# A list scheduler with due times gives way to a written order, in a kernel of memory attention and an erf-softplus FFN

## The chip, the cores and the metric

The kernel runs on 1 core of a Trainium2 chip. The metric is device time in microseconds (us) of one execution; 704.22 us is the median of three runs before the change.

## The reference, cut to what matters

```python
# q, k, v: (8 batches, 8 heads, 576, 64); phi: (8, 8, 576, 32); w_in: (512, 2048); w_out: (2048, 512)
a = exp(phi - max(phi, axis=2)); a = a / (sum(a, axis=2) + 1e-9)
k_m = einsum('bhsm,bhsd->bhmd', a, k)
v_m = einsum('bhsm,bhsd->bhmd', a, v)
scores = matmul(q, k_m.T) / sqrt(64)
attn = exp(scores - max(scores)); attn = attn / (sum(attn) + 1e-9)
x = matmul(attn, v_m)              # as (4608 tokens, 512)
h = x @ w_in
g = h * erf(softplus(h))
out = g @ w_out
```

The result is wanted in float32, so nearly every large product is made of three products of high and low parts.

## The kernel before

The kernel never forms `x`. For each batch `b` it multiplies `v_m` into `w_in` (`vw`, `vw_sums`, through `heads`, line 652: small tiles of 64 x 32) and then the attention weights with that (line 850 for batches 0 and 1, in halves of 288 tokens: `ffn1`; line 756 from batch 2 on: `quad`, seven products for two steps). A step `i` is one of 16 blocks of 128 hidden columns of one of 8 batches, 128 in all. Step by step follow `softplus`, `erf`, `g_split` (product with h, then a high and a low part) and `ffn2` (line 935: four token blocks `d` of 128 rows, accumulated in `pso` over 16 steps); the 64 tokens left over of two batches go together (`ffn2_rest`, `psr`). `memories` makes `k_m` and `v_m` (`sums`, line 598), `attention` the weights. The first four steps of `ffn1` and the first eight of `ffn2` are exact products of float32 rather than three.

The weights come from the host as 64-bit numbers of the same values. `decode` turns one block of w_in or w_out back: a "top" cast bf16 to f16 (line 485), a "low" multiply (lines 486 on ScalarE, 488 on VectorE) and a merge on VectorE (line 480). w_in is stored again in DRAM for the later batches. The pool `wo` has nine buffers for raw and split weights, and both halves of the first q.

The program is written as operations with a cost, a rank (100 x the step at which they are due, some shifted), what they read and write, and one or two "ways", engines that can do them. `Plan.order` then builds the order: a list scheduler that keeps a model of time per engine, of free buffers (`room`, `MOST`, `LEAST`) and of TensorE's clock; at each turn it takes the operation that can begin first, by rank among those that are near. On TensorE it goes on with "small" products as long as there are some. `SHIFT` moves the rank of single operations. The order of the list is the order on each engine. `fill` puts products of zeros (line 414) on TensorE where the model sees it idle in the start.

Of the kernel before, what the change touches and what calls it, by code (L numbers as in the profile page):

```python
# [41 lines left out]
SHIFT = {  # L42
    "at_sums": {
        ("s", 2): 2, ("s", 3): 2,
    },
    "attention": {
        (0,): 12, (2,): 4.5, (3,): 1,
    },
    "decode": {
        ("in", 0): -9, ("in", 1): -10.5, ("in", 2): -12, ("in", 5): -11, ("in", 7): -11, ("out", 2): 11.5,  # L50
        ("out", 3): -14, ("out", 7): -0.5,
    },
    "ffn2_rest": {
        ("s", 0, 2): 5.5, ("s", 10, 2): -5.5, ("s", 12, 2): 3.5, ("s", 6, 2): 2, (7, 0, 2): -14,
    },
    "g_split": {
# [4 lines left out]
    },  # L61
    "memories": {
        (1,): 1.5, (2,): 4,
    },
    "split_wo": {
        (0,): 13, (4,): 4.5, (6,): 6,
    },
    "vw": {
        (0, 4, False): 1.5, (0, 6, False): -9.5, (1, 1, False): 0.5, (1, 5, False): 5, (1, 6, False): -5.5,
    },  # L70
    "vw_sums": {
        ("s", 3): -6.5, (2, 0): 8, (2, 1): 2.5, (2, 3): -1,
    },
}


class Op:
    def __init__(self, ways, rank, kind, nbytes, edge):
        self.ways, self.rank, self.kind, self.nbytes, self.edge = ways, rank, kind, nbytes, edge
        self.engine = next(iter(ways))  # L80
        self.before, self.after, self.tiles, self.placed = set(), [], set(), []
        self.ready = self.start = self.end = 0.0
        self.fill = 0
# [19 lines left out]

class Plan:
# [3 lines left out]
    SIGNAL = 60.0  # L108
    TABLE = 1283.0
    SWITCH = 98.0  # L110
    RELOAD = 170.0
    NEAR = 100.0

    def __init__(self, room, any_order, least, shared):
        self.ops, self.seen = [], {}
        self.room, self.any_order, self.least, self.shared = room, any_order, least, shared
        self.pool_of, self.users, self.turn = {}, {}, {}

    def tile(self, pool, *key):
        self.pool_of[key] = pool  # L120
        self.users[key] = []
        self.turn.setdefault(pool, []).append(key)
        return key

    shift = 0

    def op(self, engine, cost, rank, reads, writes, emit, kind=None, nbytes=0, edge=None, after=(),
           holds=(), other=()):
        x = Op({engine: (cost, emit), **dict(other)}, rank, kind, nbytes, edge)
        x.shift = self.shift  # L130
        x.before.update(after)
        for w, keys in ((False, reads), (True, writes)):
            for k in keys:
                k, part = (k[0], k[1]) if isinstance(k[0], tuple) else (k, None)
                x.tiles.add(k)
# [18 lines left out]
        for k in x.tiles:  # L154
            if k in self.users:
                self.users[k].append(x)
                x.placed.append(k)
        x.placed += [k for k in holds if k not in x.tiles]
        self.ops.append(x)
        return x  # L160

    def order(self):
        n_wait = {}
        for x in self.ops:
            x.rank += 100 * x.shift
            n_wait[x] = len(x.before)
            for y in x.before:
                y.after.append(x)
        room, turn = dict(self.room), dict.fromkeys(self.turn, 0)
        left = {k: len(u) for k, u in self.users.items()}  # L170
        waiting = {e: [x for x in self.ops if e in x.ways and not n_wait[x]] for e in ENGINES}
        free = dict.fromkeys(ENGINES, 0.0)
        table, at_edge, small = None, True, False
        landed, clock, filling = 2200.0, Clock(), True
        releases, out, now, held = [], [], 0.0, set()

        def fits(x):
            need = {}
            for k in x.placed:
                if k in held:  # L180
                    continue
                p = self.pool_of[k]
                if p not in self.any_order and self.turn[p][turn[p] + need.get(p, 0)] != k:
                    return False
                need[p] = need.get(p, 0) + 1
            if any(room[p] < n for p, n in need.items()):
                return False
            return not any(p in self.least for p in need) or self.shared >= sum(
                max(n, self.room[p] - room[p] + need.get(p, 0)) for p, n in self.least.items())

        def best_way(x):
            return min(x.ways, key=lambda e: max(free[e], x.ready, now) + x.ways[e][0])

        while len(out) < len(self.ops):
            best = None
            for e, xs in waiting.items():
                can = [x for x in xs if fits(x)]
                if e == ACT and not at_edge:
                    can = [x for x in can if x.kind != "exp"]
                can = [x for x in can if len(x.ways) == 1 or best_way(x) == e]  # L200
                if not can:
                    continue
                t0 = max(free[e], now, min(x.ready for x in can))
                near = [x for x in can if x.ready <= t0 + self.NEAR]
                if e == PE and small and any(x.kind == "small" and x.ready <= t0 for x in near):
                    near = [x for x in near if x.kind == "small" and x.ready <= t0]
                x = min(near, key=lambda x: x.rank)
                t = max(free[e], x.ready, now)
                if best is None or t < best[0]:
                    best = (t, x, e)  # L210
            if releases and (best is None or releases[0][0] <= best[0]):
                now, _, p = heapq.heappop(releases)
                room[p] += 1
                continue
            if best is None:
                raise RuntimeError(f"nothing fits after {len(out)} of {len(self.ops)}")
            now, x, e = best
            x.engine, (cost, x.emit) = e, x.ways[e]
            for w in x.ways:
                waiting[w].remove(x)  # L220
            for k in x.placed:
                if k not in held:
                    held.add(k)
                    room[self.pool_of[k]] -= 1
                    turn[self.pool_of[k]] += 1
# [16 lines left out]
            elif e == ACT:  # L242
                if x.kind is not None and x.kind != table:
                    cost += self.TABLE
                    table = x.kind
                if x.edge is not None:
                    at_edge = x.edge
                late = 75.0
            elif e == DVE:
                late = 60.0  # L250
            x.cost = cost
            free[e] = now + cost
            x.start, x.end = now, now + cost + late
            if e == SP:
                begin = max(now + 900, landed)
                landed = begin + x.nbytes / (250 if x.nbytes < 1.2e5 else 340 if begin < 13000 else 385)
                x.end = landed + 900
            out.append(x)
            for y in x.after:
                n_wait[y] -= 1  # L260
                y.ready = max(y.ready, x.end + self.SIGNAL)
                if not n_wait[y]:
                    for w in y.ways:
                        waiting[w].append(y)
            for k in x.tiles:
                if k in left:
                    left[k] -= 1
                    if not left[k]:
                        end = max(u.end for u in self.users[k]) + self.SIGNAL
                        heapq.heappush(releases, (end, len(out) * 16 + len(releases), self.pool_of[k]))  # L270
# [4 lines left out]
def tile_memory_attention_then_erf_softplus_ffn(  # L275
# [11 lines left out]
    nc = tc.nc  # L287
# [20 lines left out]
    GB, WB, IB, VB = 3, NPR + 1, 3, 3  # L308
    SLOTS = 31
    MOST = {"h": 14, "e": 12, "at": 14, "sc": 4, "phiT": 3, "uv": 3, "dk": 2, "rr": 3}  # L310
# [858 lines left out]
```

## Time and profile before

| | |
|---|---|
| runs before | 704.22 us median (703.86 to 704.79) |
| the profiled execution | 704.14 us, of which 702.3 us are its span |
| TensorE, VectorE, ScalarE busy | 691.8, 581.8, 541.9 us of the span |
| granted TensorE clock, mean | 0.998 |

The span is the time from the first to the last instruction. PE is TensorE's products, PEld its weight loads, DVE VectorE, ACT ScalarE, POOL GpSimd, SP the engine whose queue issues the DMAs. In rows on instructions the columns are the start and the time in us, the engine, the line of the program, the operation, what is written from what, its shape and how many there are; in brackets the idle time of the engine ahead of it, and who ended it.

### The profile page before, as it was taken

Reading aid. Unit: us, or ns where it says so; the run is one execution under the profiler, and the core shown is the slowest. Engines: PE = TensorE matmul, PEld = TensorE weight load, DVE = VectorE, ACT = ScalarE, POOL = GpSimd, SP = SyncE. Lnnn points to the kernel's source line nnn. Section 1 sums busy time; section 2 is a strip of 40 time slices with the busy share of each in tenths; the row PEclk is TensorE's granted clock in tenths of the full one; section 3 lists DMA queues with packets and bytes.
Section 4 is the critical chain, followed back from the end, with each engine's and each line's share of the span. In section 5 each row is a group of like instructions: output and inputs, shape, how many; then the busy total and the mean of one; then the engine's idle time right before and its main releaser. Section 6 shows DMA issues by size and latency. Waiting matters only on the chain.

```text
span 702.3 us, 13828 instructions
## 1 busy us (share of the span) xinstructions
PE 691.8 (99%) x5204; PEld 549.8 (78%) x5204; DVE 581.8 (83%) x1202; ACT 541.9 (77%) x978; POOL 30.6 (4%) x70
## 2 busy tenths in 40 slices
PE   8999999999999999999999999999999999999997
PEld 3566678778878888888878888788888888888885
DVE  3999999988878889998987997789998898767750
ACT  4689987977777887888878996589987895686831
POOL 0111210000000000000000000000000000011220
PEclk9999999999999999999999999999999999999999
DMA  8999953861736336273634346445321434330002
GB/s 324 415 393 421 378 186 105 289 238 34 256 106 214 102 123 227 76 236 91 250 119 139 99 147 229 128 133 191 117 76 66 122 100 139 98 110 1 1 1 75
DMA packets 71283, 115.07 MB, mean 164 GB/s; under 512 B 38064, under 2 KB 46256, under 8 KB 71216
## 3 DMA queue, kind: packets, MB, share of 16 engines
q1 hardware_dynamic: 71216, 114.18, 47.3%
q8 instruction: 41, 0.67, 0.4%
q14 instruction: 26, 0.21, 0.1%
HBM read 93.19 MB, written 20.97 MB: 163 GB/s over the span
## 4 chain that ended last, share of the span: by engine, by line
PE 90%; DMA 3%; DVE 3%; ACT 2%; SPq 1%; issue 1%; ACTq 0%; DVEq 0%
PE pso L935 48%; PE psh L756 19%; PE psh L850 7%; PE psr L935 6%; PE psa L652 6%; PE psa L598 2%; DMA q<-qT 2%; DMA phiT<-phiT 2%; PE idle L414 1%; DVE sv L677 1%; PE psa L620 0%; ACT wv L403 0%; SPq L442 0%; DVE wv L405 0%; DVE e L887 0%
## 5 line engine op out<-in xcount | busy, mean ns | idle before, releaser
L935 PE MATMUL pso<-wo,g 128*128 128x512 f32 x1440 | 392.6, 395 | 0.0
L935 PEld LDWEIGHTS pso<-wo,g 128*128 128x128 f32 x1440 | 250.4, 188 | 41.7 <-issue 7.3
L756 PEld LDWEIGHTS psh<-at,wv 128*128 128x128 f32 x1008 | 168.6, 188 | 36.5 <-DVE h L677 1.8
L756 PE MATMUL psh<-at,wv 128*128 128x288 f32 x1008 | 190.9, 298 | 1.2 <-ACT g L904 0.4
L872 ACT ACTIVATE e<-h 128x576 f32<-128x576 f32 x128 | 87.0, 685 | 38.8 <-DVE h L677 31.0
L887 DVE TENSOR_TENSOR e<-e,h 128x576 f32<-128x576 f32 x120 | 88.9, 749 | 19.7 <-ACT e L877 19.4
L905 DVE TENSOR_TENSOR g<-e,g 128x576 fp32r<-128x576 f32 x120 | 89.7, 750 | 0.6
L877 ACT ACTIVATE e<-e 128x576 f32<-128x576 f32 x128 | 84.1, 676 | 0.4
L677 DVE TENSOR_TENSOR uv<-uv,psh 128x288 f32<-128x288 f32 x96 | 43.1, 449 | 19.0 <-PE psh L756 15.8
L677 DVE TENSOR_TENSOR h<-uv,psh 128x288 f32<-128x288 f32 x96 | 43.1, 449 | 13.6 <-PE psh L756 13.0
L904 ACT ACTIVATE g<-e 128x576 fp32r<-128x576 f32 x68 | 46.5, 684 | 8.6 <-PE pso L935 4.1
L935 PE MATMUL psr<-wo,rr 128*128 128x512 f32 x192 | 49.5, 393 | 0.0
L850 PE MATMUL psh<-at_hi,vw 128*128 128x288 f32 x224 | 45.1, 306 | 0.8 <-DVE sc L798 0.8
L771 ACT ACTIVATE uv<-psh 128x288 f32<-128x288 f32 x96 | 38.9, 405 | 8.8 <-PE psh L756 8.0
L872 ACT ACT_TABLE_LOAD x33 | 42.3, 1283 | 3.9 <-DVE h L677 3.4
L877 ACT ACT_TABLE_LOAD x33 | 42.3, 1283 | 0.6
L935 PEld LDWEIGHTS psr<-wo,rr 128*128 128x128 f32 x192 | 34.8, 188 | 6.8 <-issue 0.4
L850 PEld LDWEIGHTS psh<-at_hi,vw 128*128 128x128 f32 x224 | 35.0, 188 | 5.9 <-issue 2.1
L914 POOL CAST rr<-g 128x64 fp32r<-128x64 f32 x32 | 14.0, 447 | 579.9 <-DVE g L903 550.6
L652 PE MATMUL psa<-wi,vm 64*32 64x256 f32 x1024 | 37.1, 383 | 0.0
L984 ACT ACTIVATE ot<-pso 128x512 f32<-128x512 f32 x32 | 18.5, 604 | 20.0 <-PE pso L935 19.7
L403 ACT ACTIVATE wv<-sv 128x512 fp32r<-128x512 f32 x48 | 27.8, 624 | 5.6 <-DVE sv L677 5.3
(88 smaller groups left out, 809.8 us busy)
## 6 DMA issues: line engine op xcount, KB each, us to landing
wi<-w_in_d SPq DMA_DIRECT2D x56, 512.0 KB, 4.6
kv<-kv SPq DMA_DIRECT2D x32, 640.0 KB, 9.1
q<-qT SPq DMA_DIRECT2D x16, 576.0 KB, 6.9
out<-ot SPq DMA_DIRECT2D x32, 256.0 KB, 3.5
w<-w_in SPq DMA_DIRECT2D x8, 1023.8 KB, 14.4
w<-w_out SPq DMA_DIRECT2D x8, 1023.8 KB, 13.6
rr<-rest_d SPq DMA_DIRECT2D x28, 256.0 KB, 3.4
rest_d<-g SPq DMA_DIRECT2D x104, 64.0 KB, 1.7
```

What stands on the lines that cost most here:

```text
L403: lambda: nc.scalar.activation(get_hi(), get_src(), AF.Identity))
L652: nc.tensor.matmul(out=get(ps[par])[p * M : (p + 1) * M, m * n : (m + 1) * n], lhsT=w[rows, p, :], rhs=get(x)[rows, p, :], start=True, sto ...
L677: op(DVE, on_dve(n) + extra, rank, reads, [o], lambda: nc.vector.tensor_tensor(out=get_o(), in0=get_x(), in1=get_y(), op=kind))
L756: nc.tensor.matmul(out=get(ps[o]), lhsT=lhsT, rhs=rhs, start=(n < 4 and m == 0), stop=(m == 2), skip_group_check=n >= 4)
L771: lambda x=x: nc.scalar.activation(get(uv)[:, x], get(ps[x]), AF.Identity))
L850: nc.tensor.matmul(out=get(ps), lhsT=x[:, g, k % 2 * P : (k % 2 + 1) * P], rhs=y[:, g, :], start=(n + g == 0), stop=(n == len(parts) - 1 a ...
L872: last[:] = [op(ACT, on_act(S), rank, [("h", i)], [e], lambda: nc.scalar.activation(get(e), get(("h", i)), AF.Softplus), kind="softplus", ...
L877: last[:] = [op(ACT, on_act(S), rank, [e], [e], lambda: nc.scalar.activation(get(e), get(e), AF.Erf), kind="erf", edge=edge, after=last)]
L887: op(DVE, on_dve(S), rank, [e, h], [to if i >= FR2 else (t, 0)], lambda: nc.vector.tensor_tensor(out=get(t)[:, 0].bitcast(F32) if i < FR2 ...
L904: other={ACT: (on_act(S), lambda: nc.scalar.activation(get(t)[:, 0], get(e), AF.Identity))})
L905: op(DVE, on_dve(S), rank, [e, (t, 0)], [(t, 1)], lambda: nc.vector.tensor_tensor(out=get(t)[:, 1], in0=get(e), in1=get(t)[:, 0].bitcast(F ...
L935: nc.tensor.matmul(out=o, lhsT=y, rhs=z, start=(start and n == 0), stop=(stop and n == len(parts) - 1))
```

## The change

`Plan.order` builds no order any more. `WRITTEN` is a text of 3500 numbers in base 32. All operations are sorted by rank (no `SHIFT`); each number takes the operation at position n >> 1 of those that are left, and n & 1 says which of its ways. Models of room and of readiness go; the model of time stays, for the fillers.

Besides: the top cast of `decode` may go to ScalarE; `JOIN` ties the `sums` of batch b + 1 and the first `heads` of `vw_sums` of batch b (2 to 6) into one operation; the last store is cut in two halves of 256 columns, one evicted on ScalarE and stored by SP, one on VectorE and stored from ScalarE's queue; two planning costs are other numbers.

```diff
-SHIFT = {
...
+DIGITS = "ABCDEFGHIJKLMNOPQRSTUVWXYZabcdefghijklmnopqrstuvwxyz0123456789+-"
+WRITTEN = (
+    "lejcCAiUAACAkOGEEClEACAAheieGGCKCCOGGMNLKGJGCECECCECOSOOOUOhEhECQhAhACOcCaMChHWKhDKKEChHaMMWAjAQUZKKUhXhUESCe"
...
+def numbers(text):
+    n = 0
+    for c in text:
+        d = DIGITS.index(c)
+        n = 32 * n + d % 32
+        if d < 32:
+            yield n
+            n = 0
...
+        if join:
+            (was, first), x.rank = x.ways[engine], max(x.rank, rank)
+            x.ways[engine] = (was + cost, lambda: (first(), emit()))
...
+        left, out = sorted(self.ops, key=lambda x: x.rank), []
+        free, landed = dict.fromkeys(ENGINES, 0.0), 2200.0
+        clock, filling, small, table = Clock(), True, False, None
+        for n in numbers(WRITTEN):
+            x = left.pop(n >> 1)
+            e = list(x.ways)[n & 1]
+            cost, x.emit = x.ways[e]
+            now = max([free[e]] + [y.end for y in x.before])
...
-    MOST = {"h": 14, "e": 12, "at": 14, "sc": 4, "phiT": 3, "uv": 3, "dk": 2, "rr": 3}
-    LEAST = {"h": 4, "e": 4, "at": 7, "sc": 3, "phiT": 2, "uv": 1, "dk": 1, "rr": 2}
+    SHARED = ("h", "e", "at", "sc", "phiT", "uv", "dk", "rr")
...
         op(DVE, 1330, rank, [(key, "top")], [(key, "top")],
-           top(lambda y, x: nc.vector.tensor_copy(out=y, in_=x)))
+           top(lambda y, x: nc.vector.tensor_copy(out=y, in_=x)),
+           other={ACT: (2250, top(lambda y, x: nc.scalar.activation(y, x, AF.Identity)))})
...
+    def partner(what, b, c=0):
+        if what == "vw" and c == 0 and JOIN <= b < B - 1:
+            return small["sums", b + 1]
+        
+        return None
...
+        if o == ("psr", B - 1):
+            n = DM // 2
+            half = [slice(0, n), slice(n, DM)]
+            op(ACT, on_act(n, True), rank - 30, [o], [(t, 0)],
+               lambda: nc.scalar.activation(get(t)[:, half[0]], get(o)[:, half[0]], AF.Identity))
+            op(DVE, on_dve(n), rank - 30, [o], [(t, 1)],
+               lambda: nc.vector.tensor_copy(out=get(t)[:, half[1]], in_=get(o)[:, half[1]]))
+            to = out.rearrange("(b s) d -> b s d", b=B)[B - 2 :, S - REST :]
+            op(SP, 60, rank, [(t, 0)], [], lambda: nc.sync.dma_start(
+                out=to[:, :, half[0]], in_=get(t)[:, half[0]]), nbytes=P * n * 4)
+            op(ACT, 600, rank, [(t, 1)], [], lambda: nc.scalar.dma_start(
+                out=to[:, :, half[1]], in_=get(t)[:, half[1]]))
+            return
```

How the text is read: its first number is 190, so position 95, first way. In the sorted list the loads stand first (ranks from -2000), then `memories` (-1000), the scores (-800) and so on, and position 95 is the `zeros` memset of rank 0. The second number, 124, is position 62 of the rest, a one-column memset of a weight tile; the third and fourth, 2 and 0, are the loads of the second and the first `phiT`. So the opening reads, engine by engine (half 1 of q is u = 1):

- SP: phiT 1, phiT 0, k 0, k 1, q 0, q 1, v 1, v 0, w_in 0, 1, 2, 3, store of w_in 0, w_out 0, phiT, w_in 4, w_in 5, store of w_in 1, w_out 1, store of w_in 2, phiT, w_out 2. Before: phiT 0, 1, k 0, 1, q 0, w_in 0, v 0, 1, q 1, w_in 1, w_out 0, w_in 2, w_out 1, w_in 3, w_out 2.
- VectorE from the scores on: two transposes of half 0, one of half 1, maximum 0, transpose 1, maximum 1, subtractions 1 and 0, sum 1, small ones, sum 0, product 1, low multiply of w_in 0, product 0, merge of w_in 0, last transpose 1, low and merge of w_in 1, last transpose 0, low of w_in 2 and w_in 3, merge of w_in 2, merge of w_in 3, top cast of w_out 0.
- ScalarE: top casts of w_in 0, 1, 2 and 3, with the evictions of `heads` 0 behind the second and those of `heads` 1 behind the third.
- TensorE: both scores and the sums of v in one, `heads` of w_in 0, one `ffn1` half, `heads` of w_in 1, six halves, `heads` 3, one half, `heads` 2, eight halves of steps 4 to 7, then `ffn2` of step 0: sixteen halves ahead of the first `ffn2`, where before there were twelve.

In the whole text the second way is taken 118 times: 62 casts of g on ScalarE (before 68), 14 h of `quad` on VectorE (16), 13 h of `ffn1` on ScalarE (17), 15 low multiplies on VectorE (3), 11 top casts on ScalarE (none), 3 copies of the first `phi` on ScalarE (2). Products of small tiles stand in 45 groups, three of them ahead of the first `ffn1`. ScalarE's functions change table 90 times.

## Rows read from the trace of the kernel before

**Rows 1.** The page: the span, part 1 (busy us, share, instructions) and of part 2 what the DMA engines moved in each of 40 equal slices.

```profile
span 702.3 us, 13828 instructions
PE 691.8 (99%) x5204; PEld 549.8 (78%) x5204; DVE 581.8 (83%) x1202; ACT 541.9 (77%) x978; POOL 30.6 (4%) x70
...
GB/s 324 415 393 421 378 186 105 289 238 34 256 106 214 102 123 227 76 236 91 250 119 139 99 147 229 128 133 191 117 76 66 122 100 139 98 110 1 1 1 75
```

**Rows 2.** Busy time of each engine by stretch: the stretch, its length, busy us and instructions of each, granted clock, share of the DMA engines, GB/s.

```profile
31.15:43.20 12.05, 11.12 (x57) 9.20 (x55) 11.69 (x20) 11.16 (x19) 1.36 (x8) 1.00 1.02 375
43.20:100.00 56.80, 56.77 (x417) 35.55 (x418) 54.48 (x80) 50.33 (x81) 12.48 (x20) 1.00 0.97 365
100.00:176.00 76.00, 75.16 (x646) 62.46 (x648) 69.50 (x141) 62.70 (x103) 0.00 (x0) 1.00 0.48 160
```

**Rows 3.** TensorE's products by line over the whole span: busy us and mean ns of one, then the idle time ahead of them and who ended it.

```profile
L756 PE MATMUL psh<-at,wv 128*128 128x288 f32 x1008 | 190.9, 298 | 1.2 <-ACT g L904 0.4 <-ACT bias L521 0.3 <-DVE wv L405 0.3
L850 PE MATMUL psh<-at_hi,vw 128*128 128x288 f32 x224 | 45.1, 306 | 0.8 <-DVE sc L798 0.8
L935 PE MATMUL pso<-w,g 128*128 128x512 f32 x64 | 29.8, 600 | 1.0 <-PE psh L850 1.0
L414 PE MATMUL idle<-zeros 128*128 128x512 bf16 x76 | 20.5, 420 | 1.0 <-DVE zeros L395 1.0
```

**Rows 4.** The chain that ended last, from the last q load to the first output products: start, us, what.

```profile
6.05 13.23 DMA q<-qT
...
31.31 10.97 PE psh L850 x56
...
43.23 4.53 PE pso L935 x10
47.77 0.59 PE psa L652 x16
```

**Rows 5.** The same chain at three later places: the first and the last of the five pairs of sums and `heads`, a group of `heads` among output products, and the last such group of the span.

```profile
174.49 2.33 PE psa L598 x80
176.81 1.02 PE psa L652 x32
...
501.78 1.02 PE psa L652 x32
502.80 2.33 PE psa L598 x80
...
605.50 0.70 PE pso L935 x3
606.21 1.02 PE psa L652 x32
607.23 1.58 PE pso L935 x6
608.82 0.39 PE psh L756 x3
...
644.91 1.02 PE psa L652 x32
```

**Rows 6.** VectorE's instructions in order of time from the first scores on; then three lines of the program with minimum, median and maximum in ns, first and last start in us.

```profile
13.60 0.85 DVE L798 STREAM_TRANSPOSE sc<-psa 128x288 f32<-128x288 f32 x2 [5.36 <-PE psa L652]
16.22 1.23 DVE L480 SCALAR_TENSOR_TENSOR wi<-w 128x1024 uint32<-128x1024 uint32 x1
17.36 0.75 DVE L803 TENSOR_TENSOR sc<-sc,smx 128x576 f32<-128x576 f32 x1
...
30.03 0.72 DVE L819 STREAM_TRANSPOSE at<-sc 128x576 f32<-128x576 f32 x1
...
L485 DVE CAST w<-w x16: 1287/1320/1374, 14.4 to 84.8; 128x1024 f16<-128x1024 bf16 x16
L486 ACT ACTIVATE w<-w x13: 1154/1454/1803, 14.3 to 88.2; 128x1024 int32<-128x1024 uint32 x13
L488 DVE TENSOR_SCALAR w<-w x3: 683/684/709, 39.5 to 69.9; 128x1024 int32<-128x1024 uint32 x3
```

**Rows 7.** SP's queue: two loads with nothing issued between them, and the wait that w_in 0's landing ends on ScalarE.

```profile
26.81 0.33 SPq L442 DMA_DIRECT2D kv<-kv  x1
35.57 0.33 SPq L428 DMA_DIRECT2D w<-w_in  x1
...
14.31 1.80 ACT L486 ACTIVATE w<-w 128x1024 int32<-128x1024 uint32 x1 [1.55 <-DMA w<-w_in]
```

**Rows 8.** The end: instructions in order of time from the first of the last stores on, and two groups of evictions of 256 columns.

```profile
693.26 5.92 SPq L986 DMA_DIRECT2D out<-ot  x6
...
697.44 0.60 ACT L984 ACTIVATE ot<-psr 128x512 f32<-128x512 f32 x1 [0.78 <-PE psr L935]
...
L403 ACT ACTIVATE vw<-psa 128x256 fp32r<-128x256 f32 x28 | 9.6, 375 | 4.0 <-PE psa L652 3.9
L405 DVE TENSOR_TENSOR vw<-psa,vw 128x256 fp32r<-128x256 f32 x28 | 11.2, 416 | 0.6 <-ACT vw L403 0.5
```

**Rows 9.** ScalarE by line: the eviction of `uv`, and the largest of five groups of table loads (84 loads in all).

```profile
L771 ACT ACTIVATE uv<-psh 128x288 f32<-128x288 f32 x96 | 38.9, 405 | 8.8 <-PE psh L756 8.0
L872 ACT ACT_TABLE_LOAD x33 | 42.3, 1283 | 3.9 <-DVE h L677 3.4
```

More of the change, by code (lines that the diff above doesn't have):

```diff
@@ L1 @@
-import heapq
 from contextlib import ExitStack
@@ L37, with __init__ @@
 }
-SHIFT = {
[L43 to L56, printed above, removed]
[4 rows of a table removed]
[L61 to L74, printed above, removed]
-class Op:
[L78 to L83, printed above, removed]
+class Op:
+    def __init__(self, ways, rank, kind, nbytes):
+        self.ways, self.rank, self.kind, self.nbytes = ways, rank, kind, nbytes
+        self.before, self.end, self.fill = set(), 0.0, 0
 class Clock:
@@ L101, in to @@
         self.at = t
-class Plan:
[L108 to L114, printed above, removed]
-        self.ops, self.seen = [], {}
[L116 to L130, printed above, removed]
+DIGITS = "ABCDEFGHIJKLMNOPQRSTUVWXYZabcdefghijklmnopqrstuvwxyz0123456789+-"
@@ new lines, in numbers, with __init__, op @@
+def numbers(text):
[6 more added lines that the diff above has]
+            n = 0
+class Plan:
+    SIGNAL, TABLE, SWITCH, RELOAD = 60.0, 1283.0, 98.0, 170.0
+    def __init__(self):
+        self.ops, self.seen = [], {}
+    def op(self, engine, cost, rank, reads, writes, emit, kind=None, nbytes=0, after=(), other=(), join=None):
+        x = join or Op({engine: (cost, emit), **dict(other)}, rank, kind, nbytes)
+        if join:
+            (was, first), x.rank = x.ways[engine], max(x.rank, rank)
+            x.ways[engine] = (was + cost, lambda: (first(), emit()))
@@ L153, in op @@
         x.before.discard(x)
[L154 to L159, printed above, removed]
+        if not join:
+            self.ops.append(x)
         return x
     def order(self):
[L163 to L225, printed above, removed]
@@ L250, in order @@
                 late = 60.0
-            x.cost = cost
             free[e] = now + cost
-            x.start, x.end = now, now + cost + late
+            x.end = now + cost + late + self.SIGNAL
             if e == SP:
@@ L256, in order @@
                 landed = begin + x.nbytes / (250 if x.nbytes < 1.2e5 else 340 if begin < 13000 else 385)
-                x.end = landed + 900
+                x.end = landed + 900 + self.SIGNAL
             out.append(x)
[L259 to L270, printed above, removed]
+        assert not left
         return out
@@ L607, in one_memory @@
         cost = n_g * NC * (220 if b else 110)
-        op(PE, cost, rank, [a] + kvs, [ps], sums, kind="small", holds=[t])
+        small["sums", b] = op(PE, cost, rank, [a] + kvs, [ps], sums, kind="small")
         for n, g in enumerate(gs):
             rs = ("prs", b, g)
-            op(ACT, on_act(2 * n_x * D, True), rank, [ps, rs], [(t, n)],
+            op(ACT, on_act(2 * n_x * D, True) + 70, rank, [ps, rs], [(t, n)],
                lambda n=n, rs=rs: nc.scalar.activation(
@@ L641, in one_memory, with heads @@
                    [((name, b % 2), (g, par)) for g in gs], emit)
-    def heads(rank, memory, b, xs, n, holds, *key):
+    small = {}
+    def partner(what, b, c=0):
+        if what == "vw" and c == 0 and JOIN <= b < B - 1:
+            return small["sums", b + 1]
+        return None
+    def heads(rank, memory, b, xs, n, *key):
         ps = [tile_("ps", "psa", *key, par, shape=[P, len(xs) * n], pool="ps") for par in range(2)]
@@ L658, in emit @@
                         )
-        op(PE, 4 * n * len(xs) / 2.4, rank, [(memory, b % 2)] + xs, ps, emit, kind="small", holds=holds)
+        small[key] = op(PE, 4 * n * len(xs) / 2.4, rank, [(memory, b % 2)] + xs, ps, emit, kind="small",
+                          join=partner(*key))
         return ps
@@ L683, in vw_sums @@
         ts = [tile_("wv", "wv", b, 2 * p + j, shape=[P, 2, 7, P], dtype=F32R, pool="wv") for j in range(2)]
-        ps = heads(rank, "vm", b, [("wi", b, 2 * p + j) for j in range(2)], 256, [s] + ts, "vw", b, 2 * p)
+        ps = heads(rank, "vm", b, [("wi", b, 2 * p + j) for j in range(2)], 256, "vw", b, 2 * p)
         def a(g, r):
@@ L760, in product @@
             chain[:] = [op(PE, 3 * mm(U, False), rank + (0 if n < 4 else 60) + 0.1 * n,
-               [(w, (m, a_part)) for m in range(2)] + [at_] + ([] if n < 4 else [ps[o]]), [ps[o]], emit,
-               holds=h + [uv] if n == 0 else (), after=chain)]
+               [(w, (m, a_part)) for m in range(2)] + [at_] + ([] if n < 4 else [ps[o]]), [ps[o]], emit, after=chain)]
         def half(r, u):
@@ L788, in attention @@
         s = tile_("sc", "sc", u)
-        ps = heads(rank, "km", b, [("q", u)], U, [s], "sc", u)
+        ps = heads(rank, "km", b, [("q", u)], U, "sc", u)
         def view():
@@ L856, in emit @@
                     )
-        op(PE, (2 if exact else 6) * mm(U, exact), rank, [w] + ats, [ps], emit, holds=[h])
+        op(PE, (2 if exact else 6) * mm(U, exact), rank, [w] + ats, [ps], emit)
         def keep():
@@ L868, in tile_memory_attention_then_erf_softplus_ffn, with softplus, erf @@
     last = []
-    def softplus(rank, i, edge):
+    def softplus(rank, i):
         e = tile_("e", "e", i)
         last[:] = [op(ACT, on_act(S), rank, [("h", i)], [e], lambda: nc.scalar.activation(
-            get(e), get(("h", i)), AF.Softplus), kind="softplus", edge=edge, after=last)]
-    def erf(rank, i, edge):
+            get(e), get(("h", i)), AF.Softplus), kind="softplus", after=last)]
+    def erf(rank, i):
         e = ("e", i)
         last[:] = [op(ACT, on_act(S), rank, [e], [e], lambda: nc.scalar.activation(
-            get(e), get(e), AF.Erf), kind="erf", edge=edge, after=last)]
+            get(e), get(e), AF.Erf), kind="erf", after=last)]
     def g_split(rank, i):
```

106 lines of the change are left out of this document (71 added, 35 removed), and 4 rows, old and new, of the table SHIFT.

## The prediction

> **What bounds the kernel now.** I read the page first, then the stretches of the span, then TensorE by line, then the first 45 us engine by engine, then the end. TensorE is busy 691.8 of 702.3 us, at full granted clock [rows 1, 2], so a change can only gain where TensorE does nothing useful. There are four such places. From 0 to 31.15 us TensorE runs filler: 76 products of zeros, 20.5 us [rows 3]; the first useful FFN product starts only at 31.15, where the first stretch of [rows 2] begins (31.31 in the chain [rows 4]). After that it is idle about 3.0 us in all: 1.0 before the first output product, 0.8 and 1.2 before FFN-1 products [rows 3]. Third, each group of small-tile products (`heads`, `sums`) costs more than its work. Sixteen take 0.59 us and thirty-two 1.02, so a piece carries 0.16 us besides 0.43 per sixteen; and the six output products behind one take 1.58 us instead of 2 x 0.70: 0.18 more. One such group thus costs 0.34 us [rows 4, 5]. Fourth, the end: from the last product at 697.44 to 702.3 nothing is computed but one eviction [rows 8].
>
> Behind TensorE stands VectorE. From 31 to 100 us it is busy 66.2 of 68.9 us, ScalarE 61.5; from 100 to 176 us 69.5 and 62.7 of 76 [rows 2]. DMA is saturated up to 100 us (shares of 0.97 and 1.02) and half free afterwards [rows 2]. So a better start has to fit in VectorE and in what has landed.
>
> **Start: earlier first product.** The written list is only positions in the rank order, but it can be read by pencil (its opening stands in the section on the change). Before, q half 1 is the ninth load and lands at 6.05 + 13.23 = 19.28 us [rows 4], so VectorE has nothing but half 0's scores from 13.6 us; it then takes casts of weights between, and half 0's last transpose runs at 30.03 us, which is what releases the first product [rows 6]. After, both q halves and both v blocks go ahead of w_in 0. The bytes up to and with w_in 0 are the same as those that before had landed with q half 1, so w_in 0 lands at 19.3 instead of 14.3 [rows 7], and the later weights follow at one per 2.6 us (1.05 MB at the 393 to 415 GB/s of the second and third slice [rows 1]): w_in 1, 2, 3 at 21.9, 24.5, 27.1, then a store and w_out 0 at about 31. Half 1 of q has landed by about 13.4.
>
> VectorE starts its scores at 13.6 as before. Up to the merge of w_in 0 its list holds four transposes (0.85 per two), per half a maximum, a subtraction, a sum and a product over 576 columns, all put at the subtraction's 0.75, two small ones at an estimated 0.2, then one low-half multiply of 0.68 and the merge 1.23 [rows 6]. That is 1.70 + 2 x 3.4 + 0.68 + 1.23 = 10.4 us, to 24.0. The top cast of w_in 0 is on ScalarE there. No row shows that. The nearest are ScalarE's conversion of as many elements, 1.154 to 1.803 us, and VectorE's cast, 1.29 to 1.37 [rows 6]; the diff's own planning cost is 2250 ns. I take 2.25, and it is hidden either way: 19.3 + 2.25 = 21.6 is before 24.0. From 24.0: `heads` 0.59, two evictions of 256 columns on ScalarE at 0.375 [rows 8], so the first product starts near 25.4.
>
> What follows it up to the first output product: the old 56 products, 10.97 us [rows 4], plus 24 more (w_in 3's) at 0.39 per three [rows 5], 3.1 us, plus three groups of `heads` at 0.59 + 0.18: 2.3 us. Without a wait that ends at 41.8. Walking VectorE's list on, I find waits: the merge of w_in 3 comes at about 34 where TensorE could use it at 33, and the low parts of w_in 2's products some 0.6 us late. I put 1.2 us for these: 43.0, where before has 43.23 [rows 4] with 3.1 us of products and one `heads` (0.8 us; it is the one at 47.77 [rows 4]) less behind it. Gain 0.2 + 3.1 + 0.8 = **4.1 us**. Bounds: no wait at all 5.3; and 1.5, if waits of 3.8 us open because ScalarE, which holds the casts in front of the evictions, is later than I have it.
>
> Does the lead last? It needs VectorE to be as far with the rest some 4 us earlier. Over the whole list eleven of sixteen top casts go to ScalarE (VectorE -11 x 1.33 = -14.6 us), and low halves on VectorE go from 3 to 15 (+12 x 0.69 = +8.3); seventeen FFN-1 evictions on ScalarE become thirteen (0.41 each there [rows 9], taken as the same on VectorE, +1.6) [rows 6]. VectorE is relieved by 4.7 us, nearly all before 100 us: as much as the lead asks. ScalarE gets 11 x 1.15 to 2.25 and loses 12 x 1.44 and 4 x 0.41, so between -6 and +6 us, with 7.4 us of idle time from 31 to 100 us and 13.3 up to 176 [rows 2]. Weights: behind w_out 0 come 0.3 MB of `phiT`, w_in 4 and 5, a store and w_out 1, so that lands near 41 us, is decoded near 45, and is first wanted at 43.1 + 8 x 0.86 + 1.2 = 51. So I keep the 4.1.
>
> **Sums and first w_in products in one bundle.** All five pairs that `JOIN` ties already stand side by side: the first at 174.49, 2.33 us, then 1.02 of `heads`; the last at 501.78, 1.02 and then 2.33 [rows 5]. No switch is saved: **0**. In four of them the order turns round, so `heads` results come 2.33 us later; the bundle stands 9 to 14 us of TensorE work ahead of the first product that reads them, and this cover hides it. Without it each would cost up to 2.3 us.
>
> **Fewer small groups.** From the list: 42 groups after the first FFN product, before 43 (first at 47.77, last at 644.91 [rows 4, 5]). Three of the 42 lie before the first output product and are counted above, as is the one of 47.77; so 39 against 42, 3 x 0.34 = **1.0 us**.
>
> **Waits inside.** Of the 3.0 us of idle time, 1.0 is in the step above. Of the other 2.0 I count half as gone, **1.0 us** (0 to 2.0).
>
> **End.** The last eviction of 512 columns, 0.60 us, becomes two halves on two engines; 256 columns take 0.375 on ScalarE and 0.416 on VectorE [rows 8], so 0.2 is saved. The last two of six stores, which SP issues one after the other up to 699.18, go out some 0.5 us apart [rows 8]; on two queues that gap goes. Each has rows half as long, which no row prices. I take **0.7 us** (0.2 to 0.8).
>
> **Where a rule speaks against it.** Softplus, erf and exp each need their table; before loads 84 times, each 1.283 us, with 3.9 us of idle time ahead of all 33 of the largest group [rows 9]. Walking ScalarE's list I count 90: +7.7 us on an engine that is idle 160 us [rows 1], so 0 in the sum. The Trainium skill, in "ScalarE: Activation LUTs", "Rules for kernel authors", says to finish all of one set before switching and to budget about 2.7 us for every switch: six more would be 16 us of ScalarE. The trace shows 1.283 and no drain of that size beside it.
>
> **Sum.** 4.1 + 0 + 1.0 + 1.0 + 0.7 = 6.8 us off the profiled execution's 704.14 (span 702.3 and 1.8 around it): **697.3 us**. That execution is 0.08 below the median of 704.22, which changes nothing.
>
> **Rivals.**
> - *Everything meshes*: no waits at the start (5.3), 1.0 of groups, all 2.0 inside, 0.8 at the end: 9.1 us, 695.0; less still where the products that now start a little late behind a release, without counting as idle, come on time: 693.
> - *The lead is eaten*: VectorE, full from 13.6 to 100 us, gives out its products as late as before; only groups and end remain, 1.7 us: 702.4. For it: 96% busy. Against: the 4.7 us taken off it.
> - *Table loads bind*: the six extra loads fall between evictions (`uv`, `h`) that TensorE waits for; all 7.7 us show: 705.0. For it: ScalarE's evictions stand right on TensorE's heels (8.0 us of waits of `uv` on its products [rows 9]). Against: 160 us idle, and four PSUM buffers. By the Trainium skill's figure in the section named above it would be 16 us.
> - *Weights late* (the other side): the new order no longer counts free buffers; nine buffers hold all weights and both q halves, so a load at the head of SP's queue can wait for a merge on VectorE, and every later load behind it. Place: w_in 4 and 5 and w_out 1, 27 to 45 us. Price: one for one once w_out 1 is over 6 us late; it eats the 6.8 us at 13 us late and makes the kernel slower by more than 0.2% beyond 14. For it: SP's loads stand still from 26.81 to 35.57 before, too [rows 7]. Against: DMA had work queued and kept its full share through that [rows 2].
>
> **Chances.** Forecast as worked out 0.66 (694.5 to 700.0), everything meshes 0.15, lead eaten 0.08, table loads 0.05, weights late 0.06. About 0.2%, 1.4 us, is what a measurement of this kernel can tell from no change: 702.8 to 705.6 is the same. Lead eaten ends on both sides of that (0.05 faster, 0.03 same): faster 0.86, same 0.08, slower 0.06. The range takes in the meshing case and most of the eaten lead and leaves out the rest: 693.0 to 702.0.
>
> **What would show it.** Right: the first product of line `ffn1` near 25.4 and fewer than 50 fillers; the first output product near 43 with 80 FFN-1 products ahead of it, not 56; eleven casts f16<-bf16 on ScalarE at 1.2 to 2.3 us; 42 small groups after the start; the span's end 4.0 to 4.3 us after the last product's, where it was 4.9. Wrong: a first product after 28 us; idle time of TensorE over 5 us after it, on releases by DMA (weights late), by ScalarE behind a table load, or by VectorE in the first 100 us; a quad that waits for `wv` behind a bundle.

## The result, and the profile after

The changed kernel takes 712.24 us (median; 711.6 to 713.72) beside 704.5 for the kernel before: ratio 1.0111, 95% interval 1.009 to 1.0132. It is slower by 1.1%; 697.3 was forecast, so 15 us lie between forecast and time.

The page of the changed kernel: span, busy times and instructions of each engine. Its line numbers are its own: `heads` is 602, `sums` 540, `ffn1` 800, `ffn2` 885, the stores of `rest_d` 859, the one-column memsets of the weight tiles 367, the merge of w_in 421.

```profile
span 709.8 us, 13751 instructions
...
PE 688.2 (97%) x5187; PEld 551.9 (78%) x5187; DVE 581.9 (82%) x1211; ACT 549.9 (77%) x976; POOL 23.1 (3%) x70
```

TensorE has 3.6 us *less* to do than before [rows 1], no more than its filler shrank (20.5 to 16.3), and the span is 7.5 longer: 21.6 us without a product, where there were 10.5. So the time went into waits, and the first question is where.

The start is as forecast. TensorE from the first FFN product on (the same columns as before: start, us, then in brackets the idle time ahead and who ended it):

```profile
24.96 1.16 PE L800 MATMUL psh<-at,vw 128*128 128x288 f32 x4
...
42.17 6.33 PE L885 MATMUL pso<-w,g 128*128 128x512 f32 x14
52.59 0.84 PE L602 MATMUL psa<-wi,vm 64*32 64x256 f32 x16 [4.09 <-DVE wi L421]
53.76 1.11 PE L602 MATMUL psa<-wi,vm 64*32 64x256 f32 x16 [0.33 <-DVE wi L421]
54.80 4.46 PE L885 MATMUL pso<-w,g 128*128 128x512 f32 x8
```

The first FFN product comes at 24.96 (31.15 before [rows 2]), the first output product at 42.17 with 80 FFN-1 products done instead of 56 ([rows 4]: 43.23). Some 5 us of lead stand there. Four of them go at once, in the wait that ends at 52.59.

That wait costs more than its length. The stretches around it (the columns of [rows 2]; the last three are the granted clock, the DMA engines' share and GB/s):

```profile
40.00:52.59 12.59, 8.50 (x32) 4.56 (x31) 6.97 (x11) 9.25 (x10) 4.59 (x10) 1.00 0.94 390
54.00:56.00 2.00, 2.00 (x18) 0.69 (x3) 2.00 (x3) 1.03 (x3) 0.00 (x0) 0.50 0.94 217
56.00:58.00 2.00, 2.00 (x6) 0.91 (x5) 2.00 (x6) 2.00 (x6) 0.00 (x0) 0.91 1.03 335
```

After 4.09 us without a product the granted clock is 0.50, the lower of TensorE's two levels (1.2 GHz), and by 57 us it is back at 1.00. The 32 `heads` and eight output products behind the wait take 0.84 + 1.11 + 4.46 = 6.4 us. The same products at full clock, in experiment 3 below (its line numbers are 3 higher), where the wait is gone, take 4.8:

```profile
49.04 1.09 PE L605 MATMUL psa<-wi,vm 64*32 64x256 f32 x32
50.06 3.70 PE L888 MATMUL pso<-w,g 128*128 128x512 f32 x8
```

So about 1.6 us more go there. TensorE by line shows the wait again and the next ones (last columns: idle time before them, and who ended it):

```profile
L602 PE MATMUL psa<-wi,vm 64*32 64x256 f32 x1024 | 38.4, 388 | 5.8 <-DVE wi L421 4.9 <-ACT h L728 0.6 <-DMA wi<-w_in_d 0.3
L355 PE MATMUL idle<-zeros 128*128 128x512 bf16 x59 | 16.3, 422 | 1.0 <-DVE zeros L336 1.0
L540 PE MATMUL psa<-kv,phi 116*32 116x128 f32 x448 | 15.3, 274 | 1.3 <-ACT phi L477 1.3
L602 PE MATMUL psa<-q,km 64*32 64x288 f32 x256 | 11.6, 409 | 3.1 <-DMA q<-qT 2.9 <-ACT km L576 0.2
```

Before, `heads` waited for nothing and q for 0.4. The merge that TensorE waits for is itself held up. GpSimd in that stretch, and what VectorE's row says of its wait:

```profile
42.30 1.73 POOL L848 TENSOR_TENSOR rx<-g,rx 128x64 fp32r<-128x64 f32 x1
47.23 0.10 POOL L367 MEMSET w<- 128x1 uint16 x1 [3.20 <-DMA w<-w_out]
50.93 0.25 POOL L367 MEMSET w<- 128x1 uint16 x3 [3.60 <-DMA w<-w_in]
```

```profile
51.22 2.48 DVE L421 SCALAR_TENSOR_TENSOR wi<-w 128x1024 uint32<-128x1024 uint32 x2 [5.62 <-POOL w L367]
```

Each raw weight tile needs one column set to zero, a memset of 0.10 us. In the written order 8 of the 16 memsets stand *behind* the load of their own tile. The memset at 47.23 waits for the landing of its tile's load (w_out 2), the first of the three at 50.93 for that of another (w_in 7). The memsets of w_in 5 and 4, whose tiles had landed by 39 us, stand behind these two on GpSimd; VectorE's merges wait for them, and TensorE for the merges. GpSimd works in the order of the list, so 0.35 us of work holds VectorE for 5.6 and TensorE for 4.1.

SP's queue in the same stretch:

```profile
40.21 0.33 SPq L378 DMA_DIRECT2D phi<-phi  x1
52.65 0.38 SPq L859 DMA_DIRECT2D rest_d<-rx  x1
53.08 0.46 SPq L383 DMA_DIRECT2D kv<-kv  x1
```

A store of 64 KB of left-over tokens stands at its head for 12 us and waits for its data; loads wait behind it. These data (`rx`) are made on GpSimd, at 51.44, behind the same memsets. So some 5 of the 12 us belong to the memsets as well: in experiment 2, which puts them right, the same store goes out at 47.32.

Last, the end, in order of time, and the data moved from 695 to 710 us (40 slices of 0.375 us):

```profile
697.89 2.39 SPq L949 DMA_DIRECT2D out<-ot  x4
...
700.70 0.38 ACT L937 ACTIVATE ot<-psr 128x256 f32<-128x256 f32 x1 [0.78 <-PE psr L885]
701.11 0.62 SPq L941 DMA_DIRECT2D out<-ot  x1
701.12 0.42 DVE L939 COPY ot<-psr 128x256 f32<-128x256 f32 x1 [8.86 <-ACT ot L937]
701.58 1.14 ACTq L943 DMA_DIRECT2D out<-ot  x1
```

```profile
GB/s 0 0 0 0 0 0 0 0 0 38 360 355 404 361 377 393 366 142 0 16 27 38 27 41 27 49 46 49 49 49 46 49 46 49 49 38 0 0 0 0
```

From the last eviction's start to the end of the span it is now 709.8 - 700.7 = 9.1 us, before 702.3 - 697.44 = 4.9 [rows 8]. The four whole-row stores of 256 KB move at 355 to 404 GB/s; the two half stores, 128 KB each, at 49 at most, and need 17 slices, 6.4 us, for both. The stretches with the first of them alone, then with both (the last two columns are the share of the 16 DMA engines and GB/s):

```profile
702.00:704.30 2.30, 0.00 (x0) 0.00 (x0) 0.00 (x0) 0.00 (x0) 0.00 (x0) 1.00 0.11 28
704.40:708.40 4.00, 0.00 (x0) 0.00 (x0) 0.00 (x0) 0.00 (x0) 0.00 (x0) 0.56 0.14 48
```

A share of 0.14 is 2.2 engines of 16. Nor did two engines help with the eviction: VectorE's half begins when ScalarE's is over, 0.38 + 0.42 us where one eviction of 512 columns took 0.60. The row names ScalarE's eviction as what VectorE waited for; whether the two could run side by side is not shown.

### The profile page after: what moved, and what is told of

It reads as the page before. It is cut to its first block, busy times and chain, and to the rows that moved or that the text cites. A ratio compares the mean times of both kernels' runs of the same rounds, so it can differ in the third digit from the quotient of the medians.

```text
span 709.8 us, 13751 instructions
## 1 busy us (share of the span) xinstructions
PE 688.2 (97%) x5187; PEld 551.9 (78%) x5187; DVE 581.9 (82%) x1211; ACT 549.9 (77%) x976; POOL 23.1 (3%) x70
## 4 chain that ended last, share of the span: by engine, by line
PE 81%; DMA 10%; DVE 4%; ACT 2%; SPq 1%; issue 1%; POOL 0%; ACTq 0%; DVEq 0%
PE pso L885 45%; PE psh L707 17%; PE psr L885 6%; PE psa L602 5%; PE psh L800 5%; DMA w<-w_in 3%; PE psa L540 2%; DMA q<-qT 2%; DMA out<-ot 2%; DMA kv<-kv 1%; DVE g L855 1%; DMA wi<-w_in_d 1%; PE psa L562 0%; DVE wi L421 0%; SPq L374 0%
## 5 line engine op out<-in xcount | busy, mean ns | idle before, releaser
L885 PE MATMUL pso<-wo,g 128*128 128x512 f32 x1440 | 388.2, 395 | 0.0
L822 ACT ACTIVATE e<-h 128x576 f32<-128x576 f32 x128 | 84.1, 680 | 12.1 <-DVE h L628 7.5
L854 ACT ACTIVATE g<-e 128x576 fp32r<-128x576 f32 x62 | 42.1, 683 | 22.2 <-DVE e L837 14.9
L827 ACT ACT_TABLE_LOAD x37 | 47.5, 1283 | 0.6
L344 ACT ACTIVATE wv<-psa 128x128 fp32r<-128x128 f32 (+1 forms) x96 | 29.3, 333 | 19.9 <-PE psa L602 13.7
L822 ACT ACT_TABLE_LOAD x34 | 43.6, 1283 | 0.6
L800 PE MATMUL psh<-at_hi,vw 128*128 128x288 f32 x224 | 42.6, 302 | 0.0
L346 DVE TENSOR_TENSOR wv<-psa,wv 128x128 fp32r<-128x128 f32 (+1 forms) x96 | 32.5, 349 | 2.5 <-ACT wv L344 1.5
L346 DVE TENSOR_TENSOR wv<-sv,wv 128x512 fp32r<-128x512 f32 x48 | 32.8, 684 | 0.0
```

The costliest lines, as they stand in the source:

```text
L346: lambda: nc.vector.tensor_tensor(out=get_lo(), in0=get_src(), in1=get_hi().bitcast(F32), op=ALU.subtract))
L800: nc.tensor.matmul(out=get(ps), lhsT=x[:, g, k % 2 * P : (k % 2 + 1) * P], rhs=y[:, g, :], start=(n + g == 0), stop=(n == len(parts) - 1 a ...
L822: last[:] = [op(ACT, on_act(S), rank, [("h", i)], [e], lambda: nc.scalar.activation(get(e), get(("h", i)), AF.Softplus), kind="softplus", ...
L827: last[:] = [op(ACT, on_act(S), rank, [e], [e], lambda: nc.scalar.activation(get(e), get(e), AF.Erf), kind="erf", after=last)]
L854: other={ACT: (on_act(S), lambda: nc.scalar.activation(get(t)[:, 0], get(e), AF.Identity))})
L885: nc.tensor.matmul(out=o, lhsT=y, rhs=z, start=(start and n == 0), stop=(stop and n == len(parts) - 1))
```

## The experiments

Ratios are to the kernel before, run beside each on the same chip (703.76 to 704.02 there), with 95% intervals. "Changed" is the changed kernel.

**1. The end by itself.** The half stores cover two batches of 64 rows each; here each is issued as two, one per batch, on the same queue.

```diff
-            op(SP, 60, rank, [(t, 0)], [], lambda: nc.sync.dma_start(
-                out=to[:, :, half[0]], in_=get(t)[:, half[0]]), nbytes=P * n * 4)
...
+            op(SP, 60, rank, [(t, 0)], [], lambda: [nc.sync.dma_start(
+                out=to[x, :, half[0]], in_=get(t)[x * REST : (x + 1) * REST, half[0]]) for x in range(2)],
+               nbytes=P * n * 4)
...
```

> The changed kernel, but each of its two last half stores goes out as two stores, one per batch (64 rows of 1 KB), on the same two queues. Theory: the last stores are slow (46 GB/s, 7 us from the second one's issue to its landing) because the outermost dimension of their access is the 2 batches. Then the end from the last product to the end of the span falls from 9.1 to about 4.5 us and the time from 712.2 to about 707.6. Rival: it is the second queue, whose store begins only when SP's is through; then 3 us of it stay and the time is 710 to 712.

709.21 us, 1.0077 (1.0045 to 1.0109), 3.0 less than changed: below the rival's range and above the 707.6. In its profiled execution the end takes 713.2 - 708.59 = 4.6 us, so its 9.1 is cured. Data moved there from 705 to 714 us, in slices of 0.225 us, the last stores in the second group:

```profile
GB/s 0 0 0 0 0 0 0 337 355 373 364 373 391 355 400 355 392 410 355 201 0 0 36 200 55 127 219 219 187 123 0 0 0 0 0 0 0 0 0 0
```

That execution was the slowest of the six, 714.94 us: TensorE waits 5.8 us for q in it, and its mean granted clock is 0.990.

**2. The memsets.** Each late memset is put straight ahead of its tile's load; all else as in changed.

```diff
...
-    for x in plan.order():
+    listed = plan.order()
+    for x, m in memset_of.items():
+        if listed.index(m) > listed.index(x):
+            listed.remove(m)
+            listed.insert(listed.index(x), m)
+    for x in listed:
```

> The changed kernel, but each one-column memset of a weight tile that the written order puts behind the load of its tile on GpSimd (8 of 16) is put straight ahead of that load. Theory: GpSimd waits in one of them for the landing of w_out 2 and then w_in 7 (50.8 us), and behind it stand the memsets of w_in 4 and 5, so their merges and the products of line heads come 4 to 5 us late, and the stores of rest behind SP's head hold the loads back up to 52.6 us. Then the wait at 47.9 us goes, most of the waits for q at 99 and 138 us too, and the time falls by 5 to 7 us to 705 to 707. Rival: w_in 4 and 5 are late by VectorE, which is full; then at most 1 us goes: 711.

707.51 us, 1.0046 (1.003 to 1.0063): 4.7 less than changed. Of the waits of `heads` for a merge 0.5 us is left in its profile, where there were 4.9. The memsets' places cost a little less than the 5 to 7 us expected of them.

**3. Both.**

> Both edits at once: memsets ahead of their loads and the last stores by batch. Theory (two separate causes that add up): 712.2 - 4.6 - 6 = about 701.6, below the kernel before. Rival (the earlier start is eaten by VectorE anyway, and what is won at one place waits at the next): 705 to 708.

703.42 us, 0.9998 (0.9976 to 1.002). Expected were 701.6, or 705 to 708 by the rival; the measured time lies between. Two causes are gone and the time is that of the kernel before, not the 697 of the forecast: something else eats the lead. TensorE in this kernel (numbers of lines in experiments 3, 5 and 6 are 3 higher than in changed), and SP around its largest wait:

```profile
L605 PE MATMUL psa<-q,km 64*32 64x288 f32 x256 | 11.6, 409 | 4.0 <-DMA q<-qT 3.6 <-ACT km L579 0.2 <-PE psa L605 0.2
...
91.98 2.22 PE L888 MATMUL pso<-wo,g 128*128 128x512 f32 x9
96.53 0.72 PE L605 MATMUL psa<-q,km 64*32 64x288 f32 x16 [2.33 <-DMA q<-qT]
```

```profile
79.61 0.40 SPq L371 DMA_DIRECT2D w<-w_out  x1
87.27 0.37 SPq L862 DMA_DIRECT2D rest_d<-g  x1
...
89.49 0.47 SPq L391 DMA_DIRECT2D q<-qT  x1
...
SPq L862 <- DVE g L858: 195.7, 39, 12.9
```

From 79.6 to 87.3 SP stands before a store of left-over tokens; the load of q behind it goes out at 89.49 and lands 6.9 us later, at 96.4, which is when TensorE's wait ends. The last row is SP's queue over the span: 195.7 us, in 39 waits, in front of such stores for the low part of g from VectorE. Before it was 147.4 in 42. With all their other waits added, SP stands 331 us in front of these stores here and stood 312 before. So the standing itself is old; what is new is that TensorE comes to the loads behind it first.

**4. The end on the old order.** The kernel before with only its last store cut in column halves, on two engines and two queues.

> The kernel before, with its own order, and of the change only the last store in two column halves on two queues. Theory: 704.5 + 4.2 = 708.7, since the end costs 9.1 instead of 4.9 us whatever stands ahead of it. Rival (as predicted at first, the halves save 0.7 us, and the slow end in the changed kernel comes from its order): 703.8.

709.15 us, 1.0062 (1.0044 to 1.0081). On the old order the new end costs 5.4 us, so it is slow by itself and not by the written order. Data moved from 693 to 708 in it:

```profile
GB/s 0 0 0 218 393 88 0 0 38 377 355 393 361 404 169 0 0 22 44 33 35 33 41 16 11 41 46 49 49 46 49 49 46 49 38 0 0 0 22 0
```

**5. The stores of left-over tokens off SP's queue.** Experiment 3, with these stores issued by GpSimd from step 8 on (104 of 112).

```diff
-            op(SP, 60, rank, [src], [("rest", b // 2, k, b % 2)], lambda: nc.sync.dma_start(
+            op(SP, 60, rank, [src], [("rest", b // 2, k, b % 2)], lambda: (nc.gpsimd if i >= FR2 else nc.sync).dma_start(
```

> e3_both, but the stores of the left-over rows (rest_d, from step 8 on) are issued by GpSimd instead of SP; their places in the list stay. Theory: what eats the earlier start in e3_both is that loads of q, kv and w_in stand in SP's queue behind such stores, which wait for VectorE; TensorE's idle time on releases by DMA there is 6.4 us after the start (q 3.6, kv 2.2, wi 0.6). Then most of it goes and the time falls from 703.4 to 698 to 700. Rival: the loads are late because their buffers come free late, or because VectorE is behind: 702.5 to 704.

693.82 us (693.01 to 694.29), 0.9851 (0.9835 to 0.9867): 9.6 less than experiment 3, more than expected, and faster than both kernels. The same places of its trace:

```profile
span 692.4 us, 13823 instructions
...
PE 685.1 (99%) x5187; PEld 550.8 (80%) x5187; DVE 581.8 (84%) x1211; ACT 548.9 (79%) x976; POOL 99.2 (14%) x174
...
L605 PE MATMUL psa<-q,km 64*32 64x288 f32 x256 | 11.5, 409 | 0.2 <-ACT km L579 0.2
...
L862 POOL DMA_DIRECT2D rest_d<-g x104 | 75.8, 730 | 450.0 <-DVE g L858 241.8 <-DVE uv L631 29.6 <-DVE h L817 20.5
```

```profile
78.66 0.38 SPq L371 DMA_DIRECT2D w<-w_out  x1
79.09 0.49 SPq L377 DMA_DIRECT2D phiT<-phiT  x1
85.09 0.33 SPq L444 DMA_DIRECT2D wi<-w_in_d  x1
85.84 1.56 SPq L391 DMA_DIRECT2D q<-qT  x1
...
93.60 0.72 PE L605 MATMUL psa<-q,km 64*32 64x288 f32 x16
```

The load of q goes out 3.7 us earlier and TensorE takes it at 93.60 without a wait; no wait for a load is left among its rows. GpSimd now does the waiting, 241.8 us of it for the same values, and TensorE waits for nothing of GpSimd's. Against the span before, 9.9 us are gone: 3.9 of filler (20.5 to 16.6), 2.8 of other busy time, 3.2 of idle time.

**6. The casts back on VectorE.** Experiment 3 with the eleven top casts on VectorE at the same places.

> e3_both, but the eleven top casts that the list gives to ScalarE are done on VectorE, at the same places of the list. Theory: the early start needs VectorE relieved (11 x 1.3 us more on it now, nearly all before 90 us), so the first FFN product moves from 25 to 28 us or later, and the lead over the kernel before, 4 to 5 us at 50 to 90 us, falls below 1 us: 705 to 708. Rival: it is the order of the loads alone that gives the lead, and VectorE keeps up: 703.4.

712.14 us, 1.0104 (1.0082 to 1.0126): 8.7 more than experiment 3, outside what was expected. TensorE at its first FFN product and first output product, and by line:

```profile
27.36 1.16 PE L803 MATMUL psh<-at,vw 128*128 128x288 f32 x4
...
47.99 3.70 PE L888 MATMUL pso<-w,g 128*128 128x512 f32 x8
...
L605 PE MATMUL psa<-wi,vm 64*32 64x256 f32 x1024 | 37.8, 386 | 5.4 <-DVE wi L424 4.4 <-DMA wi<-w_in_d 0.8 <-ACT h L731 0.2
```

In experiment 3 the first FFN product comes at 25.78 and the first output product at 42.94, 5 us earlier. VectorE is what the start hangs on, and the lead is bought by the casts that leave it.

**7. The bundles turned round.** Experiment 3 with `heads` ahead of `sums` in each of the five bundles.

```diff
-            x.ways[engine] = (was + cost, lambda: (first(), emit()))
+            x.ways[engine] = (was + cost, lambda: (emit(), first()))
```

> e3_both, but in the five bundles of JOIN the products of heads go first and the sums of the next batch second. Theory: a bundle waits for the later of its inputs; in e3_both one waits 1.1 us at 415 us for the exponentials that only the sums read. With heads first 1.0 us of work lies ahead of that wait: 0.5 to 1.2 us less, 702.4. Rival: the bundle costs nothing either way: 703.4.

702.0 us, 0.9975 (0.9957 to 0.9992). That is 1.4 us less than experiment 3, but the two intervals overlap (0.9976 to 1.002 there). Whether the order inside the bundle is worth the 0.5 to 1.2 us expected or nothing, these runs can't tell.

**8. The move on the old order.**

> The old list order with one edit: the stores of the 64 left-over tokens from step 8 on are issued by GpSimd, not by SP. If the move is a gain of its own, whatever the order, this falls as far as it made the written order fall, by 9.6 us, to about 694. If the move only lets the written order keep its lead, there is little for it to give here, since TensorE of the kernel before is idle for 2 us after its start: 702.5 to 704.5.

704.45 us, 1.001 (1.0001 to 1.002). No gain, though SP's waits in front of these stores fall from 312 to 6 us. In these two orders the move pays only where loads wait at SP long enough to reach TensorE; in the kernel before TensorE waits 1.6 us in all for loads, by its own waits (us in all, times, longest):

```profile
PE psa L598 <- DMA kv<-kv: 1.2, 2, 0.9
...
PE psa L652 <- DMA q<-qT: 0.4, 1, 0.4
```

**9. The whole store again.** Experiment 5 with the end of the kernel before: one eviction, two stores of whole rows on SP.

> The written order with the early memsets and the moved stores, and the last store as in the kernel before: one eviction of 512 columns on ScalarE, two stores of 64 whole rows on SP. If the cost of the end lies in the outermost size 2 of the half stores alone, the stores split by batch have given all of it back and this comes within 0.5 us of 693.8. If half rows cost by themselves, it is faster by more than 0.5, below 693.3. If the two-engine eviction is worth the 0.7 that the prediction gave it, it is slower, at 694.5.

694.19 us, 0.9859 (0.9844 to 0.9874), 0.4 from experiment 5. Half rows in themselves cost nothing that shows, and two engines and two queues give nothing.

**10. Changed, with only the stores moved.**

> The changed kernel with only the stores of the left-over tokens from step 8 on moved to GpSimd. If the three causes add up (the end 4.5 us, the memsets behind their loads about 5.5, the rest for SP's queue), this is 693.8 + 4.5 + 5.5 = 703.8, and TensorE still waits about 4 us near 48 us. If the wait near 48 us was itself made by SP's queue standing still, it goes as well and the time is about 698.3.

704.67 us, 1.0004 (0.9991 to 1.0017), 0.9 above the sum of three separate causes and 6 above the other case. So the wait near 48 us was not made by SP's queue, at most lengthened by it. The wait of `heads` for merges is still there, in TensorE's waits (us in all, times, longest):

```profile
PE psa L602 <- DVE wi L421: 3.3, 3, 2.8
```

From 52 to 56 us the granted clock is 0.50 here too.

**11. Whole rows on two queues.**

> As the run with the old end, but the second of the two last stores goes out from ScalarE's queue. If the gap of 0.5 us between the two issues on SP is on the path, as the prediction took it, this is 0.3 to 0.5 us faster than that run. If ScalarE's own issue (1.1 us in the changed kernel) stands in its place, it is the same or slower by up to 0.6.

694.72 us, 0.9864 (0.9838 to 0.9891), no faster than experiment 9. SP's gap of 0.5 us between two issues buys nothing when the second store leaves from ScalarE's queue.

## Why the prediction was wrong

Three costs were missing. In the order in which the runs take them away: the memsets 4.7 us (712.24 to 707.51), the end 4.1 (to 703.42), SP's queue 9.6 (to 693.82), 18.4 in all. What each is worth depends on what is left beside it: the end is 3.0 in experiment 1's median, 4.5 by its length in the profiles (9.1 to 4.6) and 5.4 on the old order; the stores' move alone, experiment 10, is 7.6. Without the three the written order is worth 10.2 us, more than the 6.8 of the sum.

- **Start: right.** 24.96 for 25.4, 42.17 for 43.0, and the lead of 4.1 was rather 5. The sign "fewer than 50 fillers" was wrong (59), the time they take was not in the sum.
- **"Does the lead last?": the step that failed, twice.** "So I keep the 4.1" put every wait behind the start at nothing, and "waits inside" even took 1.0 off. It looked at VectorE and at three weight loads. Both were sound as far as they went: experiment 6 shows that VectorE's relief is what carries the lead. The 4.7 us of it are 4.3 in the first 100 us (busy 85.2 before, 80.9 changed) and nothing over the span (581.8 and 581.9), in part because the sum left out the six casts of g that come back to VectorE (26.1 us of them for 23.4). It didn't look at GpSimd, which [rows 1] show busy 4% of the span; but the diff's own reading names a memset among the first operations, and the list gives where the others stand. An instruction of 0.10 us holds whoever waits for it, if the one ahead of it waits for a DMA: 4.9 us of TensorE's waits on merges where there were none, and about 1.6 us of lower clock, which no term had. Nor did it follow SP's queue beyond 45 us: with 5 us of lead q, kv and w_in are wanted earlier, whereas a store at the head of the queue goes when its data come. TensorE's waits for loads are 6.4 us in experiment 3 and none in experiment 5. [rows 7] showed SP standing still for 8.8 us; the argument against, that DMA had work queued through that stretch, holds in changed only up to the wait: the DMA engines' share is 0.79 from 52.6 to 100 us.
- **The rival *weights late*** had the right place (w_in 4 and 5) and the right queue, and a wrong culprit: w_in 4 and 5 had landed and waited for a memset, and SP stands 7 us in all in front of weight loads in changed, but 333 in front of the stores.
- **End: wrong, +4.2 where -0.7 stood.** "Rows half as long, which no row prices" was the warning, and the bounds (0.2 to 0.8) left out a loss. Experiment 4 shows that the new end is slow on the old order too, experiment 9 that half rows cost nothing, experiment 1 that one store per batch takes the cost away: it was the shape of the access, two batches outermost. That the halves would be evicted side by side was wrong as well (0.80 us for 0.60). The Trainium skill, "DMA: Bandwidth & Descriptors", section "Why a DMA increments its semaphore by 16 and not by 1", says that a DMA is spread over the largest number of engines, at most 16, that divides the slowest dimension of its accesses which isn't 1. Outermost 2 would be two of 16 engines; the trace agrees, with a share of 0.14, 2.2 engines. An estimate from that page and the 404 GB/s of the whole-row stores is an eighth, 50; the trace has 49. Split by batch the outermost size is 64, and the end falls to 4.6. The rule also has the lowest-numbered engines taken, which would make the two half stores share the same two; the trace agrees in that the share hardly grows (0.11 to 0.14) when the second store joins and both together stay at 49.
- **Casts on ScalarE: mis-sized, without an effect that shows.** The eleven take 2545 ns each, above the upper bound of 2.25:

```profile
L827 ACT ACT_TABLE_LOAD x37 | 47.5, 1283 | 0.6
...
L427 ACT ACTIVATE w<-w 128x1024 f16<-128x1024 bf16 x11 | 28.0, 2545 | 0.0
```

- **Table loads: right.** The 90 are there, at 1283 ns, 0.6 us of idle time ahead of the largest group; ScalarE's busy time rose by 8.0 us and experiment 5 is fast with the same loads.
- **Bundles 0: not contradicted** (experiment 7). **Groups: the count is right**, 42 after the first FFN product where there were 43; the 1.0 us put on it no run shows by itself. **Waits inside:** in experiment 5 what is left after the start is 0.3 us for a merge; the 2.0 were nearly all to be had, once nothing new waits.

What stays open: how much of the 9.6 us of experiment 5 belongs to which load (q, kv, w_in and `phiT` all stand behind the moved stores), since each wait that goes shifts the next; and why the profiled execution of experiment 1 waits 5.8 us for q where changed waits 2.9.

## What to carry to other kernels

When work is pulled forward, follow every in-order queue that feeds it to its end, also that of an engine that is 4% busy: one entry that waits for late data or for a DMA holds all entries behind it, and a store whose data come late belongs on a queue on which nobody waits. A store's outermost dimension decided here how fast it moved; read the shape of the access before counting on two queues. An order that gains at the start must be asked, load by load, whether its loads go out earlier too.

## What the runs showed of the hardware that was not expected

- A store of 128 KB with two outermost steps moved at 28 GB/s alone, and two of them on two queues at 48 together, with a DMA share of 0.11 and 0.14; the same bytes with 64 outermost steps moved at up to 219 GB/s (experiment 1).
- After 4.09 us without a product TensorE's granted clock was 0.50 (1.2 GHz) for more than 3 us, and the products behind the wait took 6.4 us where they take 4.8.
- ScalarE's conversion of 128x1024 bf16 to f16 took 2.55 us, VectorE's 1.32 [rows 6].
- GpSimd was busy 0.73 us with each store it issued, and 104 of them hurt nothing in experiment 5.
